# Gated linear attention into an expert layer: the third unit's k product moves to VectorE and the first 300 entries of the order are written anew

## The chip, the cores and the metric

The kernel runs on 1 core of one Trainium2 chip. The metric is the device time of one execution in microseconds. A core has five engines with a queue each: TensorE (PE in the profile, with its weight loads as PEld), VectorE (DVE), ScalarE (ACT), GpSimd (POOL) and SyncE (SP, which here only issues transfers). Every queue is worked in its order, and the engines meet by semaphores.

## The reference, cut to what matters

Gated linear attention over 4 batches, 8 heads, 768 positions and 48 channels, then a two-layer expert network over the 3072 x 384 result:

```python
for t in range(S):
    state = f[:, :, t, :, None] * state + np.einsum('bhd,bhe->bhde', k[:, :, t], v[:, :, t])
    y[:, :, t] = np.einsum('bhd,bhde->bhe', q[:, :, t], state)
...
h = x @ w_in                       # 3072 x 384 by 384 x 2048
relu6 = np.clip(h + 3.0, 0.0, 6.0)
g = h * relu6 / 6.0
return g @ w_out                   # 2048 x 384
```

Here `f` is the sigmoid of `f_logit`, and `x` is `y` with the heads side by side.

## The kernel before, in words

**Units.** The recurrence is done in chunks of 128 positions: 4 batches by 6 chunks are 24 units, named 0 to 23; units 0 to 3 are the first chunks of the four batches. For a unit, `load` brings the gates (258.5 KB), `loadk` and `loadq` bring k and q (256 KB each; from unit 2 on `loadq` brings both, 512 KB) and `loadv` brings v (200 KB). `gate` is the sigmoid on ScalarE. On VectorE `back` scans the gates backwards (L433), `kmul` multiplies k by that scan (L446), `rend` takes a reciprocal (L451), `fwd` scans forwards (L457) and `qmul` multiplies q (L463). On TensorE `tk` transposes k (L529), `att` makes the scores (L510), `kv` the unit's sum of k and v (L550), `qs` the part that comes from the state before (L585), `av` the part from the scores (L601), and `xs` takes back the rounded part of the result (L626). Between these, `ktok`, `carry0`, `carry1`, `xh` and `xl` are copies out of PSUM on ScalarE for units 0 to 3 (L536, L563, L570, L622, L634), and `mask` multiplies the scores on VectorE (L517). `hole` issues two small transfers that move rows of the result within SBUF (L643).

**Weights.** Each of 16 slices of the two weight matrices is brought by `ld` (768 KB) and split by `cy`, `z` and `high` on ScalarE (L296, L287, L316) and `mid`, `dif`, `top` and `lowi`/`lowo` on VectorE (L300, L307, L311, L319).

**Expert network.** Group c holds the 512 results of the units 4c to 4c+3. For group 0 the first slices are done by halves: `mm1a.f` needs units 0 and 1 alone, `mm1b.f` units 2 and 3 (L846); then `relua`/`relub` on ScalarE (L855), `ga`/`gb` on VectorE (L859) and `mm2a`/`mm2b` on TensorE (L864). Later slices and groups use L678, L727, L738 and L790. `mm1a` multiplies by the high half of a slice's weights in its first six products and by the low half, which `lowi` makes, in the last three.

**Where the order comes from.** Nothing is scheduled while it runs. The string `ORDER` lists 1565 entries, and the program issues them in that order, so each engine's queue is the list's entries for that engine. The string `ON_POOL` names the entries that go to GpSimd in place of VectorE. An entry `warm.n` multiplies a tile of zeros, n blocks of 128 columns, into an unused PSUM bank (L1089): these are the blank products. A number behind a product's name picks its PSUM bank; two steps of a unit that use the same pair of banks wait for each other in the order of the list.

**Queue of SP.** All input transfers and the holes stand in one queue. A transfer waits there for its buffer: `load.3` for `fwd.0`, which frees the first of three gate buffers, and `hole.0` for `xl.0`. Whatever stands behind waits with it.

Of the kernel before, what the change touches and what calls it, by code (L numbers as in the profile page):

```python
# [58 lines left out]
rend.2 cy.0 load.3 warm.3 kv.1.3 z.0 mid.0 loadq.2 kmul.2 gate.3 end.2 back.3 ld.1 carry0.1 warm.1 qs.1.0 dif.0 fwd.2
qmul.2 top.0 xl.0 carry1.1 loadq.3 loadv.2 av.1 hole.0 tk.2.4 rend.3 xh.1 xs.1 xl.1 z.1 warm.5 att.2.2 kmul.3 cy.1  # L60
mid.1 fwd.3 ktok.2 high.0 warm.4 kv.2.1 carry0.2 end.3 tk.3.4 ktok.3 mask.2 load.4 gate.4 qs.2.0 hole.1 av.2 xh.2
carry1.2 lowi.0 mm1a.0.4 relua.0 dif.1 qmul.3 top.1 high.1 ga.0 loadv.3 xs.2 att.3.2 mask.3 kv.3.1 ld.2 carry0.3
carry1.3 lowi.1 xl.2 loadq.4 warm.1 qs.3.2 av.3 xh.3 mm1a.1.4 cy.2 xs.3 xl.3 relua.1 z.2 back.4 kmul.4 rend.4 fwd.4
ga.1 decay.4 mm2a.0 qmul.4 load.5 gate.5 tk.4.1 mm2a.1 ktok.4 loadv.4 ld.3 cy.3 z.3 hole.2 mid.2 dif.2 top.2 att.4.2
kv.4.3 hole.3 mm1b.0.0 high.2 back.5 mid.3 relub.0 loadq.5 mm1b.1.1 relub.1 lowi.2 gb.0 dif.3 kmul.5 rend.5 gb.1
mm1a.2.4 mm1b.2.0 top.3 mm2b.0 mm2b.1 fwd.5 tk.5.1 relua.2 relub.2 gb.2 qmul.5 ld.4 z.4 cy.4 mid.4 mm2b.2 high.3 ktok.5
lowi.3 ga.2 mm1b.3.0 load.6 gate.6 loadq.6 dif.4 back.6 top.4 load.7 mm1a.3.4 ld.5 relub.3 mm2a.2 relua.3 ga.3 high.4
gb.3 cy.5 z.5 mask.4 mm2a.3 lowi.4 mm1a.4.1 relua.4 rend.6 ld.6 mm1b.4.4 relub.4 loadv.6 gate.7 loadq.7 mm2b.3 carry0.4
kmul.6 fwd.6 mid.5 ga.4 dif.5 z.6 qmul.6 top.5 cy.6 tk.6.1 ktok.6 mm2a.4 back.7 ld.7 decay.5 high.5 qs.4.2 decay.6
att.5.0 gb.4 av.4 kv.6.1 carry1.4 lowi.5 mm1.5.4 mask.5 mm2b.4 carry0.6 xh.4 z.7 xl.4 mid.6 dif.6 kmul.7 carry1.6  # L70
loadv.5 kv.5.3 ld.8 relu.5 g.5 mm2x.5 cy.7 top.6 high.6 cy.8 rend.7 tk.7.0 mid.7 dif.7 load.8 lowi.6 carry0.5 top.7
mm1.6.4 ktok.7 qs.5.2 fwd.7 qmul.7 high.7 loadv.7 relu.6 g.6 z.8 decay.7 att.6.0 ld.9 lowi.7 gate.8 av.5 cy.9 z.9
mask.6 mm1.7.4 relu.7 mid.8 dif.8 top.8 mid.9 carry1.5 dif.9 high.8 low.8 mm2x.6 mm1.8.0 g.7 loadq.8 ld.10 top.9 xh.5
cy.10 relu.8 high.9 back.8 rend.8 mm2x.7 ld.11 xl.5 g.8 att.7.2 z.10 cy.11 qs.6.0 kv.7.3 mid.10 load.10 loadv.8 av.6
dif.10 low.9 top.10 z.11 mid.11 gh.8 mm1.9.4 ld.12 ld.14 xh.6 xl.6 gl.8 mm2.8 dif.11 high.10 low.10 relu.9 g.9 cy.12
mm1.10.1 top.11 mask.7 kmul.8 carry0.7 gh.9 gl.9 hole.4 relu.10 high.11 mm2.9 carry1.7 g.10 low.11 z.12 mid.12 ld.13
dif.12 top.12 cy.13 gh.10 gl.10 tk.8.1 ktok.8 mm1.11.0 z.13 high.12 qs.7.2 mm2.10 av.7 loadq.9 ld.15 kv.8.3 decay.8
relu.11 mid.13 dif.13 low.12 loadv.9 mm1.12.1 g.11 gh.11 xh.7 top.13 carry0.8 high.13 xl.7 hole.7 gl.11 relu.12 z.14
z.15 low.13 fwd.8 qmul.8 mm2.11 g.12 gh.12 mm1.13.4 relu.13 g.13 cy.14 gh.13 gl.13 gl.12 mm2.12 cy.15 qs.8.2 mid.14
dif.14 att.8.0 mask.8 lowo.0 top.14 high.14 hole.6 hole.5 mm1.16.4 load.9 mid.15 mm1.17.1 relu.16 carry1.8 relu.17  # L80
dif.15 ws1.0 g.16 mm1.20.0 g.17 loadq.11 low.14 gate.10 xtop.0 gate.9 mm1.18.1 load.11 top.15 relu.18 loadq.10 back.9
high.15 gh.16 av.8 back.10 mm1.14.4 g.18 mm2.13 lowo.4 gh.17 relu.14 low.15 g.14 gh.14 mm1.15.1 mm1.19.4 lowo.6 gh.18
kmul.9 gl.18 rend.9 relu.15 g.15 lowo.3 gh.15 gl.14 gl.15 tk.9.1 lowo.5 lowo.1 mm2.14 fwd.9 mm2.15 gl.16 ktok.9 gl.17
# [1173 lines left out]
```

## Time and profile before

| | us |
|---|---|
| median of 3 runs | 455.48 (455.41 to 456.07) |
| the profiled execution, its own time | 455.55 |
| its span from the first to the last instruction | 453.8 |
| TensorE busy in the span | 446.9 |
| VectorE busy | 357.8 |
| ScalarE busy | 231.5 |
| GpSimd busy | 19.8 |

The 1.75 us between the span and the execution's own time lie before the first and behind the last instruction. The profile says of each engine when it worked, how long it stood idle before an instruction, and what released it; the chain of waits goes back from the last instruction to what released each step. Times in the rows are us from the span's start.

### The profile page before, as it was taken

Reading aid. Unit: us, or ns where it says so; the run is one execution under the profiler, and the core shown is the slowest. Engines: PE = TensorE matmul, PEld = TensorE weight load, DVE = VectorE, ACT = ScalarE, POOL = GpSimd, SP = SyncE. Lnnn points to the kernel's source line nnn. Section 1 sums busy time; section 2 is a strip of 40 time slices with the busy share of each in tenths; the row PEclk is TensorE's granted clock in tenths of the full one; section 3 lists DMA queues with packets and bytes.
Section 4 is the critical chain, followed back from the end, with each engine's and each line's share of the span. In section 5 each row is a group of like instructions: output and inputs, shape, how many; then the busy total and the mean of one; then the engine's idle time right before and its main releaser. Section 6 shows DMA issues by size and latency. Waiting matters only on the chain.

```text
span 453.8 us, 12556 instructions
## 1 busy us (share of the span) xinstructions
PE 446.9 (98%) x5447; PEld 290.3 (64%) x5447; DVE 357.8 (79%) x639; ACT 231.5 (51%) x393; POOL 19.8 (4%) x31
## 2 busy tenths in 40 slices
...
GB/s 285 248 264 408 173 224 228 196 172 0 73 139 66 190 20 110 58 6 118 91 0 85 109 129 1 30 135 1 2 10 1 7 28 1 1 116 2 1 0 74
DMA packets 25819, 43.18 MB, mean 95 GB/s; under 512 B 2592, under 2 KB 17440, under 8 KB 25760
## 3 DMA queue, kind: packets, MB, share of 16 engines
q1 hardware_dynamic: 24160, 41.56, 27.0%
...
q14 instruction: 16, 0.13, 0.1%
...
## 4 chain that ended last, share of the span: by engine, by line
PE 95%; DMA 2%; DVE 1%; POOL 1%; issue 0%; SPq 0%; ACT 0%; DVEq 0%; POOLq 0%
PE o L727 36%; PE pair L790 16%; PE single L790 9%; PE pair L678 7%; PE single L678 5%; PE o L864 3%; PE pair L510 3%; PE pair L585 3%; PE pair L601 3%; PE pair L550 2%; PE o L738 2%; DMA qkf<-qk 2%; PE pair L529 2%; PE pair L880 1%; PE o_half L880 1%; PE single L846 1%
## 5 line engine op out<-in xcount | busy, mean ns | idle before, releaser
L727 PE MATMUL o<-gg,weight 128*128 128x512 f16 x744 | 173.5, 379 | 0.0
L727 PEld LDWEIGHTS <-weight 128*128 128x128 f16 x744 | 71.7, 98 | 73.7
L790 PEld LDWEIGHTS <-weight 128*128 128x128 f16 x672 | 65.0, 98 | 13.2
L790 PE MATMUL pair<-xmem,wide 128*128 128x256 f16 x384 | 51.4, 273 | 0.2 <-issue 0.2
L701 ACT ACTIVATE gg<-raws 128x512 f16<-128x512 f32 x64 | 38.5, 624 | 22.8 <-PE o_half L880 7.2
L790 PE MATMUL single<-xmem,weight 128*128 128x256 f16 x384 | 49.8, 273 | 0.0
L819 ACT ACTIVATE raws<-pair,half 128x512 f32<-128x512 f32 x32 | 21.5, 684 | 43.0 <-PE pair L790 34.0
L790 PEld LDWEIGHTS <-wide 128*128 128x128 f16 x384 | 36.8, 98 | 9.2 <-DVE single L805 0.7
L819 ACT ACTIVATE raws<-single,half 128x512 f32<-128x512 f32 x32 | 22.0, 687 | 38.5 <-PE single L790 37.6
L678 PEld LDWEIGHTS <-weight 128*128 128x128 f16 x243 | 23.1, 98 | 26.7 <-issue 0.3
L790 PE MATMUL pair<-xmem,weight 128*128 128x256 f16 x288 | 36.5, 273 | 0.0
L711 DVE TENSOR_TENSOR gg<-raws,gg 128x512 f16<-128x512 f32 x48 | 31.9, 682 | 5.2 <-ACT gg L701 5.1
L824 DVE SCALAR_TENSOR_TENSOR raws<-raws,single 128x512 f32<-128x512 f32 x32 | 21.8, 682 | 17.6 <-ACT raws L819 17.6
L678 PE MATMUL pair<-xmem,weight 128*128 128x512 f16 x144 | 33.2, 379 | 0.0
L805 DVE TENSOR_TENSOR pair<-pair,raws 128x512 f32<-128x512 f32 x16 | 11.2, 697 | 26.7 <-PE pair L790 23.7
L457 DVE TENSOR_TENSOR_SCAN suffix<-gates,rend 112x516 f32<-112x516 f32 x24 | 29.7, 1236 | 1.2 <-POOL qkf L446 1.1
L824 DVE SCALAR_TENSOR_TENSOR raws<-raws,pair 128x512 f32<-128x512 f32 x32 | 21.4, 681 | 10.9 <-ACT raws L819 10.8
L433 DVE TENSOR_TENSOR_SCAN suffix<-gates,unit 112x516 f32<-112x516 f32 x23 | 28.0, 1222 | 0.2 <-ACT gates L427 0.2
L678 PE MATMUL single<-xmem,weight 128*128 128x512 f16 x99 | 23.2, 380 | 0.0
L688 ACT ACTIVATE tg<-pair,half 128x512 f32<-128x512 f32 x16 | 10.9, 689 | 19.4 <-PE pair L678 16.2
L701 ACT ACTIVATE gg<-tg 128x512 f16<-128x512 f32 x24 | 14.4, 626 | 9.0 <-DVE tg L692 5.2
L517 DVE TENSOR_TENSOR a<-pair,causal 128x512 f32<-128x512 f32 x24 | 16.3, 683 | 1.3 <-PE pair L550 1.0
(135 smaller groups left out, 638.4 us busy)
## 6 DMA issues: line engine op xcount, KB each, us to landing
...
qkf<-qk SPq DMA_DIRECT2D x22, 512.0 KB, 4.8
gates<-fg SPq DMA_DIRECT2D x23, 258.5 KB, 3.2
...
outT<-os SPq DMA_DIRECT2D x11, 256.0 KB, 2.9
qkf<-qk SPq DMA_DIRECT2D x4, 256.0 KB, 4.1
...
```

Source lines behind the costliest of these rows:

```text
L433: nc.vector.tensor_tensor_scan(flat(sf)[:, ::-1], gt[:, 1:][:, ::-1], flat(unit)[:, ::-1], 0.0, op0=ALU.mult, op1=ALU.add,)
L457: nc.vector.tensor_tensor_scan(flat(sf), gt[:, :NP * (C + 1)], flat(rend), 0.0, op0=ALU.mult, op1=ALU.add,)
L510: nc.tensor.matmul(d["at"][HC * odd:HC * (odd + 1), e, 2 * n + c], t[rs, 1, n, c, odd], t[rs, 0, n, c, odd], start=not growing[at], stop=T ...
L517: nc.vector.tensor_tensor(d["a"].rearrange("r p e t -> r e p t"), d["at"], causal.unsqueeze(1).unsqueeze(1).broadcast_to([128, 2, NP, HC]) ...
L585: nc.tensor.matmul(d["y"][to:to + m, odd, n, cs], before[rs, p, :m], t[rs, 0, n, c, odd], start=alone and (odd, e) not in seen, stop=False ...
L678: nc.tensor.matmul(h, win[:, f, a, k * 128:(k + 1) * 128], g["xt"][:, k, :g["n"] // C, b], start=i == 0, stop=i == 3 * KT - 1,)
L701: nc.scalar.activation(as_t(d, 0), d["t"], AF.Copy)
L711: engine("gl", int(g["name"]) * NF + f).tensor_tensor(as_t(d, 1), d["t"], as_t(d, 0), op=ALU.subtract)
L727: nc.tensor.matmul(g["o"][m], wout[:, f, a, m * 128:(m + 1) * 128], g[f]["gg"][:, b], start=f == 0 and i == 0, stop=f == NF - 1 and i == 2 ...
L790: nc.tensor.matmul(to[:, n * 256:(n + 1) * 256], weights(q, n, a), g["wide"][:, :, block - 3, b], start=fresh and count == 1, stop=count = ...
L819: nc.scalar.activation(to, src, AF.Relu, bias=half, scale=RISE)
L824: nc.vector.scalar_tensor_tensor(to, to, TOP, src, op0=ALU.min, op1=ALU.mult)
```

## The change: what it does

`kmul.2`, the product of k with the backward scan for unit 2, is struck from `ON_POOL`, so it runs on VectorE. The first 309 entries of `ORDER` are the same entries in another order, but for the blank products: after the first ten blocks there were 23 in nine places, now 18 in nine places. The 1256 entries behind are untouched.

```diff
 ON_POOL = """
-kmul.2 decay.4 kmul.6 lowi.5 kmul.7 decay.7 lowi.7 kmul.8 gl.9 decay.8 gl.11 qmul.8 gl.12 lowo.0 low.14
+decay.4 kmul.6 lowi.5 kmul.7 decay.7 lowi.7 kmul.8 gl.9 decay.8 gl.11 qmul.8 gl.12 lowo.0 low.14
 """.split()
 ORDER = """
-load.0 loadh.0 gate.0 gateh.0 back.0 backh.0 loadk.0 load.1 loadv.0 loadq.0 rend.0 end.0 kmul.0 fwd.0 gate.1 back.1
+load.0 loadh.0 gate.0 gateh.0 loadk.0 back.0 backh.0 rend.0 kmul.0 warm.10 end.0 fwd.0 load.1 gate.1 back.1 loadq.0
...
```

**VectorE, from unit 1's `kmul` on.** Before (`rend.1`, `kmul.1`, `mask.0`, `fwd.1`, `qmul.1`, `back.2`, `mask.1`, `rend.2`, `mid.0`, `back.3`, `dif.0`, `fwd.2`):

```order
L451 RECIPROCAL rend<-suffix_79 112x4
L446 TENSOR_TENSOR qkf_184<-qkf_184,suffix_79 112x512
L517 TENSOR_TENSOR a_217<-pair_70,causal 128x2x4x64
L457 SCALAR_TENSOR_TENSOR suffix_79<-gates_78,rend 112x516
L463 TENSOR_TENSOR qkf_184<-qkf_184,suffix_79 112x512
L433 SCALAR_TENSOR_TENSOR suffix_81<-gates_80,unit 112x516
L517 TENSOR_TENSOR a_271<-pair_70,causal 128x2x4x64
L451 RECIPROCAL rend<-suffix_81 112x4
L300 TENSOR_SCALAR raws<-top_274 128x768
L433 SCALAR_TENSOR_TENSOR suffix_77<-gates_76,unit 112x516
L307 TENSOR_TENSOR top_274<-top_274,raws 128x768
L457 SCALAR_TENSOR_TENSOR suffix_81<-gates_80,rend 112x516
```

and now (`rend.1`, `kmul.1`, `fwd.1`, `mask.0`, `back.2`, `qmul.1`, `rend.2`, `kmul.2`, `fwd.2`, `mask.1`, `qmul.2`, `back.3`):

```order
L451 RECIPROCAL rend<-suffix_79 112x4
L446 TENSOR_TENSOR qkf_154<-qkf_154,suffix_79 112x512
L457 SCALAR_TENSOR_TENSOR suffix_79<-gates_78,rend 112x516
L517 TENSOR_TENSOR a_228<-pair_70,causal 128x2x4x64
L433 SCALAR_TENSOR_TENSOR suffix_81<-gates_80,unit 112x516
L463 TENSOR_TENSOR qkf_154<-qkf_154,suffix_79 112x512
L451 RECIPROCAL rend<-suffix_81 112x4
L446 TENSOR_TENSOR qkf_224<-qkf_224,suffix_81 112x512
L457 SCALAR_TENSOR_TENSOR suffix_81<-gates_80,rend 112x516
L517 TENSOR_TENSOR a_311<-pair_70,causal 128x2x4x64
L463 TENSOR_TENSOR qkf_224<-qkf_224,suffix_81 112x512
L433 SCALAR_TENSOR_TENSOR suffix_77<-gates_76,unit 112x516
```

`kmul.2` (the second L446) is new here, `fwd.1` stands ahead of `mask.0`, `fwd.2` ahead of `mask.1`, and the first slice's `mid.0` and `dif.0` stand behind `mask.2`. Further down, `back.4` stands ahead of `ga.0` and `lowi.1`, where it stood behind them.

**SP, from the ninth transfer to the first `hole`** (`qkf` is k and q, `gates` the gates, `v` v, `raws` a weight slice, `xmem` a hole). Before:

```order
L408 DMA gates_80<-fg 128x517
L419 DMA qkf_184<-qk 128x512
L283 DMA raws<-w 128x3072
L423 DMA v_268<-v 128x400
L408 DMA gates_76<-fg 128x517
L412 DMA qkf_304<-qk 128x1024
L283 DMA raws<-w 128x3072
L412 DMA qkf_327<-qk 128x1024
L423 DMA v_329<-v 128x400
L643 DMA xmem<-xmem 16x3x256 x2
```

and now:

```order
L419 DMA qkf_154<-qk 128x512
L408 DMA gates_80<-fg 128x517
L412 DMA qkf_224<-qk 128x1024
L423 DMA v_253<-v 128x400
L408 DMA gates_76<-fg 128x517
L283 DMA raws<-w 128x3072 x2
L423 DMA v_377<-v 128x400
L412 DMA qkf_415<-qk 128x1024
L643 DMA xmem<-xmem 16x3x256 x2
```

Unit 2's k and q (`loadq.2`, the first row of 128x1024) come tenth in the queue, ahead of the first weight slice, where they came thirteenth; the two first slices stand together behind `load.3`.

**TensorE, unit 0's scores and the part from the state.** Before:

```order
L510 MATMUL pair_70<-qkf_137 64x64 [waits DMAHW5_49,DVE_49,Activation_49]
L510 MATMUL pair_70<-qkf_137 64x64 x15
L585 MATMUL pair_71<-qkf_137,middle_102 64x64 [waits Pool_49]
L585 MATMUL pair_71<-qkf_137,middle_102 64x64 x7
L1089 MATMUL idle<-blank 128x128
L601 MATMUL pair_71<-a_217,v_140 64x64 [waits PE_49,DVE_49]
```

and now:

```order
L510 MATMUL pair_70<-qkf_135 64x64 [waits DMAHW4_49,DVE_49]
L510 MATMUL pair_70<-qkf_135 64x64 x15
L1089 MATMUL idle<-blank 128x128
L585 MATMUL pair_71<-qkf_135,middle_102 64x64 [waits Activation_49,Pool_49]
L585 MATMUL pair_71<-qkf_135,middle_102 64x64 x7
L529 MATMUL single<-ident,qkf_154 128x112 [waits DMAHW6_49,DVE_49]
```

The wait on ScalarE (for `carry0.0`) has gone from `att.0` to `qs.0`: `carry0.0` now comes behind `att.0` in the list, and as both use the same pair of banks, it waits for `att.0`. Unit 1's transposition (`tk.1`, L529) stands ahead of `av.0`.

## Rows read from the trace of the kernel before

**Rows 1.** The page's head, and its part 1: busy time by engine

```profile
span 453.8 us, 12556 instructions
PE 446.9 (98%) x5447; PEld 290.3 (64%) x5447; DVE 357.8 (79%) x639; ACT 231.5 (51%) x393; POOL 19.8 (4%) x31
```

**Rows 2.** Windows: length, busy us by engine, granted clock, DMA share, GB/s

```profile
5.00:30.00 25.00, 23.25 (x580) 16.52 (x580) 23.25 (x36) 17.21 (x37) 2.93 (x2) 1.00 0.83 309
30.00:450.00 420.00, 419.70 (x4865) 271.95 (x4863) 331.96 (x594) 211.95 (x354) 14.17 (x13) 1.00 0.25 82
```

**Rows 3.** The chain of waits, 0 to 110 us: start, length, what

```profile
7.53 7.28 DMA qkf<-qk
...
14.95 2.43 POOL qkf L446
```

**Rows 4.** Timeline of TensorE and its loads: start, length, what, idle before

```profile
9.37 0.44 PE L585 MATMUL pair<-qkf,middle 48*64 48x64 f32 x16
...
14.16 1.33 PE L550 MATMUL pair<-v,ktok 64*64 64x48 f32 x48
...
21.10 0.91 PE L550 MATMUL pair<-v,ktok 64*64 64x48 f32 x48
...
28.08 1.16 PE L846 MATMUL single<-xmem,weight 128*128 128x256 f16 x9
```

**Rows 5.** Timeline of VectorE: `kmul.1`, `fwd.2`, `lowi.1`

```profile
8.79 0.66 DVE L446 TENSOR_TENSOR qkf<-qkf,suffix 112x512 f32<-112x512 f32 x1
...
17.41 1.23 DVE L457 TENSOR_TENSOR_SCAN suffix<-gates,rend 112x516 f32<-112x516 f32 x1 [1.07 <-POOL qkf L446]
...
26.45 0.55 DVE L319 TENSOR_TENSOR weight<-wide,weight 128x384 f16<-128x384 f32 x1
```

**Rows 6.** VectorE by line to 28.2 us: count, busy us, mean ns, idle before

```profile
L457 DVE TENSOR_TENSOR_SCAN suffix<-gates,rend 112x516 f32<-112x516 f32 x4 | 4.9, 1230 | 1.1 <-POOL qkf L446 1.1
L433 DVE TENSOR_TENSOR_SCAN suffix<-gates,unit 112x516 f32<-112x516 f32 x4 | 4.9, 1222 | 0.2 <-ACT gates L427 0.2
L517 DVE TENSOR_TENSOR a<-pair,causal 128x512 f32<-128x512 f32 x4 | 2.7, 687 | 0.3 <-PE pair L510 0.3
...
L446 DVE TENSOR_TENSOR qkf<-qkf,suffix 112x512 f32<-112x512 f32 x4 | 2.7, 672 | 0.0
```

**Rows 7.** DMA issues at 4.57 (`loadq.1`), 7.16 (`load.3`), 7.53 (`loadq.2`): KB, us to landing

```profile
qkf<-qk SPq DMA_DIRECT2D x1, 256.0 KB, 4.7
...
gates<-fg SPq DMA_DIRECT2D x1, 258.5 KB, 5.2
...
qkf<-qk SPq DMA_DIRECT2D x1, 512.0 KB, 7.3
```

**Rows 8.** Timeline of ScalarE: `carry0.0`, `z.1`, `cy.1`, `xl.3`

```profile
8.27 0.33 ACT L563 ACTIVATE middle<-pair 112x192 f32<-112x192 f32 x1 [1.21 <-PE pair L550]
...
18.86 0.91 ACT L287 ACTIVATE wide<-raws 128x768 int32<-128x768 uint32 x1
19.68 0.91 ACT L296 ACTIVATE top<-raws 128x768 int16<-128x768 int16 x1
...
29.50 0.59 ACT L634 ACTIVATE xmem<-pair 112x512 f16<-112x512 f32 x1
```

**Rows 9.** Timeline of TensorE's weight loads inside `kv.1`: start, length, idle before

```profile
14.15 0.65 PEld L550 LDWEIGHTS pair<-v,ktok 64*64 64x64 f32 x35 [0.55 <-issue]
15.05 0.31 PEld L550 LDWEIGHTS pair<-v,ktok 64*48 64x48 f32 x13 [0.24 <-issue]
```

**Rows 10.** DMA queues in 12.5 to 13 and in 16.5 to 17 us: packets, MB, share

```profile
q8 instruction: 1, 0.02, 12.0%
...
q8 instruction: 1, 0.02, 15.7%
```

**Rows 11.** Window 16 to 18 us, and SP's first `hole`

```profile
16.00:18.00 2.00, 1.69 (x53) 1.31 (x54) 0.93 (x2) 1.17 (x3) 1.37 (x1) 1.00 0.34 119
...
16.38 2.20 SPq L643 DMA_DIRECT2D xmem<-xmem  x2
```

More of the change, by code (lines that the diff above doesn't have):

```diff
@@ L59 @@
[L59 to L83, printed above, removed]
@@ new lines @@
+att.2.2 z.0 back.3 av.1 xh.1 warm.3 xs.1 z.1 mask.2 xl.1 mid.0 rend.3 end.3 dif.0 top.0 cy.1 loadv.2 warm.3 kv.2.1
+carry0.2 warm.1 qs.2.0 high.0 loadq.3 kmul.3 av.2 tk.3.4 fwd.3 carry1.2 mid.1 qmul.3 dif.1 xh.2 hole.0 ktok.3 lowi.0
+att.3.2 ld.2 cy.2 loadv.3 load.4 hole.1 gate.4 xs.2 kv.3.1 carry0.3 top.1 mm1a.0.4 high.1 mask.3 loadq.4 back.4 relua.0
+ga.0 lowi.1 load.5 xl.2 rend.4 carry1.3 qs.3.2 av.3 xh.3 mm1a.1.4 relua.1 ld.3 xs.3 xl.3 loadv.4 kmul.4 fwd.4 z.2 ga.1
+qmul.4 mm2a.0 hole.2 hole.3 mid.2 loadq.5 dif.2 top.2 ld.4 tk.4.1 ktok.4 mm2a.1 carry1.1 loadq.6 gate.5 cy.3 back.5
```

146 lines of the change are left out of this document (83 added, 63 removed).

## The prediction

> **What bounds the kernel now.** I read the page's head first: TensorE is busy 446.9 us of a span of 453.8 [rows 1]. The windows say where it is not: from 30 to 450 us it stands idle 0.3 us in all, while from 5 to 30 us it is busy 23.25 of 25 [rows 2], and 23 blank products stand among that work. So from 30 us on the time is a queue of TensorE that never runs dry, and the opening sets when that queue starts. The chain of waits names the opening's links: unit 2's k and q are issued at 7.53 and land 7.28 later, GpSimd multiplies k for 2.43, and TensorE can only then transpose it [rows 3].
>
> That gives a mark by which both orders can be compared: the start of `mm1a.1`, the first-half product of slice 1, at 28.08 [rows 4]. The same products of TensorE stand ahead of it in both orders, blanks apart, and behind it the old order has no idle time worth a name. The time changes by as much as this mark moves, plus what idle time the new order brings in behind it.
>
> **The change on VectorE.** Before, the chain from `kmul.1` at 8.79 to the end of `lowi.1` at 27.00 takes 18.21 [rows 5]. Of that 1.07 is `fwd.2` waiting for GpSimd's `kmul.2` [rows 5], about 0.3 `mask.0` waiting for `att.0`, and 0.15 one `back` [rows 6]: 1.5 in all. The new order adds `kmul.2` (0.67 by its line, 0.60 from start to start) and puts `back.4` ahead (1.22 by its line, 1.17 net) [rows 6]. If VectorE never waits, `lowi.1` ends at 8.79 + 18.21 - 1.5 + 0.60 + 1.17 = 27.3, and `ga.0`, which frees the bank for `mm1a.1`, half a microsecond earlier, at 26.8. `lowi.1` itself is wanted only by the seventh of that step's nine products.
>
> Does VectorE have to wait for `loadq.2`, now that a late landing stops its whole queue? The nine transfers that now stand ahead of `loadq.2` are the nine that ended with `loadq.1` before, and that one landed at 4.57 + 4.7 = 9.3. The 512 KB behind it take up to 2.4 (before, `loadq.2` landed at 7.53 + 7.3 = 14.8 behind `load.3` at 7.16 + 5.2 = 12.4) [rows 7]: 11.7. VectorE comes to `kmul.2` at 8.79 + 0.60 (`kmul.1`) + 1.2 (`fwd.1`) + 0.6 (`mask.0`) + 1.2 (`back.2`) + 0.7 (`qmul.1`, `rend.2`) = 13.1. So it does not wait, with 1.4 to spare, and `kmul.2` is done at 13.7 where GpSimd ended at 17.38. The 2.43 on GpSimd itself vanish; nothing else there is due before 29.
>
> **The change on TensorE and ScalarE.** `carry0.0` ran at 8.27, ahead of the scores [rows 8]; now it waits for `att.0`, which ends at 9.6, so `qs.0` starts at about 10.2 in place of 9.37 [rows 4]. That costs nothing by itself: `av.0` needs `mask.0`, which now ends at 11.2, behind `fwd.1`. From there, with steps as long as in the old order (0.45 for `qs`, 0.5 `tk`, 0.65 `att` and `av`, 0.85 net for `kv`, about 0.55 for a copy on ScalarE) and 0.15 from a releaser to a start: `att.1` at 13.2 (`qmul.1`), `tk.2` 13.95, `kv.1` 14.45, `qs.1` 15.95 (`carry0.1`), `att.2` 16.4 (`qmul.2`), `av.1` to 17.7. Then ScalarE sets the pace: `xh.1` to 18.3, `z.1` (0.91 [rows 8], some 0.8 net) to 19.1, and only then `xl.1` to 19.65, which `kv.2` has to wait for, since both use one bank. `kv.2` starts at 19.85 in place of 21.10 [rows 4]: 1.25 earlier. From `kv.2` to the mark the old order takes 28.08 - 21.10 = 6.98; the new one has the same products and waits some 0.15 more (`kv.3` for `ktok.3`), so `av.3` ends at 27.0. But `relua.0` stands on ScalarE behind `cy.2`, `gate.4`, `carry0.3` and `high.1`; it ends at 26.65, `ga.0` at 27.15, and the mark comes at 27.3. That is 0.8 earlier than before. The five blanks less are no gain of their own: they filled waits.
>
> Behind the mark `mm1b.0` needs the last `hole`, and this needs `xl.3`, at 29.50 before [rows 8] and 1.4 behind the mark's start. In the new order `relua.1` stands ahead of it: 0.05 given back, so 0.75 is left. Later places where VectorE could be late (`lowi.2`, `ga.2`, `lowi.3`, `ga.3`, `lowi.6`) come out in time by 0.2 to 1.0 by the same sums, as VectorE is itself some 0.9 ahead there: I cost them at nothing. If that cover fails, each pays its own lateness once.
>
> **The instruction read.** Inside `kv.1` TensorE stands idle 0.24 for nothing but "issue", at 14.8 to 15.05 [rows 9], and `kv.1` takes 1.33 where `kv.2` takes 0.91 [rows 4]. The only thing in flight that fits is a 16 KB read in the instruction queue, begun between 12.5 and 13 while the DMA engines were full [rows 10]. I take it that TensorE ran out of code. By counting instructions in both orders the same place comes 25 instead of 35 matmuls into `kv.1`, at 14.45 + 0.43 = 14.9. If the read arrives as before, at 15.05, that costs 0.15; if it is asked for by TensorE's own progress, it may be late by what `qs.0` is late, 0.83, and costs 15.9 - 14.9 = 1.0. Nothing lets me choose, so I take the middle, 0.55; `mask.2` has 0.2 of slack against it, so 0.35 goes on to the mark.
>
> The Trainium skill, "Runtime: NRT & Kernel Launch", section "Instruction fetch mechanics", says that the sequencer reads the next 16 KiB block with a queue of its own while it executes the current one, and that a crossing is mostly hidden. The packet's size agrees; the idle 0.24 [rows 9] speaks against "hidden" in this place. By the page the read would cost 0 and the sum would be -0.75.
>
> **The sum.** -0.75 + 0.35 = -0.4 against the profiled execution's 455.55: 455.15. The median of the runs shown is 0.07 below that execution, so **455.1**. A measurement of this kernel can tell about 0.2%, 0.9 us, from no change; this forecast is the same as before by that measure.
>
> **Rivals.**
> - *The opening runs as smoothly as its order allows.* The read is hidden, and `top.1` to `ga.0` keep ahead of TensorE, so that `av.3` and not `ga.0` sets the mark: 27.0, or 1.1 earlier, 454.4. For it: in the sums `ga.0` misses by only 0.3, and VectorE alone would have it at 26.8. Against it: every link has to be on time. 0.26. (The page of the Trainium skill named above, "Runtime: NRT & Kernel Launch", would have the read so; the gap before is the evidence against it.)
> - *The reads get slower, because the pause goes.* Before, SP waited for `xl.0` until 16.38 to issue the first `hole`, the transfers ran out, and the DMA share fell to 0.34 in 16 to 18 us; TensorE's second read, begun between 16.5 and 17, fell into that pause [rows 10, 11]. Now `xl.0` is done about 13.9 (`av.0` from 11.4, then `xh.0`, `xs.0`, `xl.0`), SP goes on, and the pause closes. The first read then costs the full 1.0, less 0.2 of slack; the second, wanted inside `kv.2` at 20.1 and asked for at 15.9, may take as long as from `qs.0`'s start at 9.37 to the first one's 15.05, 5.7, and arrive at 21.6: 1.5 more. -0.75 + 0.8 + 1.5 = +1.55: 457.0 at most, 456.5 if the second loses 1.0. It is slower by over 0.2% once both together put more than 1.65 on the path. For it: 0.24 was lost already. Against it: no later step before shows such a gap, and the packet itself takes one engine only 0.12 x 16 x 0.5 = 0.96 us [rows 10]. 0.12.
> - *`kmul.2` now blocks VectorE.* If `loadq.2` lands as late as before, at 14.8, VectorE idles 1.7 at 13.1 with `fwd.2`, `mask.1` and `qmul.2` behind it: -0.4 + 1.7 = +1.3, 456.4. It decides from a landing at 13.1 on, and is slower by over 0.2% from 14.4. Against it: 1226 KB less stand ahead of it. 0.06.
> - *Nothing is gained*, as VectorE's places behind 30 us give the 0.4 back one by one: 455.5. 0.10.
>
> **How the numbers follow.** Forecast 0.46, no gain 0.10: within 0.2%, 0.56. Smooth: 0.26 faster. The two mishaps: 0.18 slower. The range reaches from just under the smooth case to the lighter end of the slow ones: 454.3 to 456.4.
>
> **What would show it.** Right: `kmul.2` on VectorE near 13.1 with no wait before it; `fwd.2` at 13.7; `kv.2` near 19.9 behind `xl.1`; `mm1a.1` near 27.3 to 27.6; no idle time of TensorE from 30 to 450 us. The read shows as an "issue" gap in `kv.1`, 0.15 to 1.0 long. Wrong: an idle VectorE before `kmul.2` (a DMA as releaser); "issue" gaps in `kv.1` and `kv.2` that sum over 1.65; `mm1a.1` before 27.1; or idle time of TensorE before L846, L864 and L678 behind 30 us with VectorE or ScalarE as releaser.

## The result and the profile after

The changed kernel takes 458.9 us in the median of 6 runs (458.02 to 460.69) beside 455.43 for the kernel before: a ratio of 1.0082, 95% interval 1.0064 to 1.0099. It is 3.5 us slower. 455.1 was predicted, between 454.3 and 456.4. The profiled execution of the changed kernel took 458.96, its span 457.2, against 455.55 and 453.8; the sums below are made between these two.

First the windows, as in [rows 2], with single microseconds added. Columns: stretch, length, busy us of TensorE, its weight loads, VectorE, ScalarE and GpSimd (count of instructions), TensorE's granted clock, DMA share, GB/s.

```profile
5.00:30.00 25.00, 22.26 (x515) 15.77 (x514) 21.24 (x31) 14.86 (x30) 0.00 (x0) 0.86 0.83 307
30.00:450.00 420.00, 419.25 (x4896) 271.85 (x4899) 333.37 (x587) 213.46 (x357) 17.45 (x14) 1.00 0.25 80
...
17.00:18.00 1.00, 1.00 (x41) 0.70 (x33) 1.00 (x3) 1.00 (x2) 0.00 (x0) 1.00 0.83 240
20.00:21.00 1.00, 0.09 (x3) 0.00 (x0) 0.96 (x2) 0.40 (x1) 0.00 (x0) 1.00 0.74 272
22.00:23.00 1.00, 0.81 (x18) 0.48 (x18) 1.00 (x2) 0.96 (x2) 0.00 (x0) 1.00 0.62 173
23.00:24.00 1.00, 0.93 (x32) 0.95 (x32) 0.86 (x3) 0.10 (x1) 0.00 (x0) 0.52 1.03 412
28.00:29.00 1.00, 1.00 (x12) 0.69 (x7) 0.28 (x1) 0.67 (x2) 0.00 (x0) 0.50 0.03 10
30.00:31.00 1.00, 0.91 (x42) 0.70 (x44) 0.31 (x1) 0.82 (x2) 0.00 (x0) 1.00 0.00 0
```

The granted clock between 5 and 30 us is 0.86 where it was 1.00: TensorE all but stands from 20 to 21 us, runs on at full speed, and at 23.0 the clock falls to 0.50, that is to 1.2 of 2.4 GHz, until 29.9. The DMA engines, which had a pause before [rows 11], are 0.83 busy in 17 to 18 us.

TensorE's timeline, to be read against [rows 4] (start, length, line, operation, count, idle time before and its releaser). Idle time marked "issue" is time in which the engine waited for nothing that the profile shows; a *stop*, below, is such idle time of TensorE.

```profile
14.76 0.91 PE L550 MATMUL pair<-v,ktok 64*64 64x48 f32 x48
...
19.55 0.55 PE L550 MATMUL pair<-v,ktok 64*64 64x48 f32 x20 [0.21 <-ACT xmem L634]
21.27 0.66 PE L550 MATMUL pair<-v,ktok 64*64 64x48 f32 x28 [1.17 <-issue]
...
23.07 1.13 PE L601 MATMUL pair<-a,v 64*64 64x64 f32 x32 [0.18 <-DVE top L307]
...
26.73 1.53 PE L550 MATMUL pair<-v,ktok 64*64 64x48 f32 x48
...
31.24 1.16 PE L846 MATMUL single<-xmem,weight 128*128 128x256 f16 x9
```

`kv.1` runs through. `kv.2` starts at 19.55 behind ScalarE's `xl.1`, as planned, and stops for 1.17 after 20 of its 48 matmuls. At the lower clock `kv.3` takes 1.53 where `kv.2` took 0.91 before. The mark, `mm1a.1`, comes at 31.24 in place of 28.08.

VectorE's and SP's timelines (`kmul.2` and `fwd.2`; the first `hole`, `ld.2`, `loadv.3`, `load.4`):

```profile
13.01 0.66 DVE L446 TENSOR_TENSOR qkf<-qkf,suffix 112x512 f32<-112x512 f32 x1
13.70 1.23 DVE L457 TENSOR_TENSOR_SCAN suffix<-gates,rend 112x516 f32<-112x516 f32 x1
...
14.33 1.36 SPq L643 DMA_DIRECT2D xmem<-xmem  x2
15.73 0.58 SPq L283 DMA_DIRECT2D raws<-w  x1
16.36 0.43 SPq L423 DMA_DIRECT2D v<-v  x1
16.89 0.38 SPq L408 DMA_DIRECT2D gates<-fg  x1
```

The DMA view of 12.5 to 13 and of 18.5 to 19 us has the first two instruction reads, as [rows 10]:

```profile
q8 instruction: 1, 0.02, 12.6%
...
q8 instruction: 1, 0.02, 11.1%
```

The second read began at 18.8; before, it began at 16.9 [rows 10].

**Where the time went.** The profiled executions differ by 3.41: the mark by 3.16, and 0.25 behind it, where one wait of 0.30 for VectorE's `th` is new:

```profile
55.97 2.10 PE L678 MATMUL single<-xmem,weight 128*128 128x512 f16 x9 [0.30 <-DVE th L859]
```

Before, TensorE reached matmul 20 of `kv.2` at 21.10 + 20 x 0.017 = 21.44 and needed 28.08 - 21.44 = 6.64 from there to the mark. Now it passed that place at 21.27, only 0.17 earlier, although `kv.2` had started 1.55 earlier: the stop took the lead. From there it needed 31.24 - 21.27 = 9.97 for the same products: 3.33 more. -0.17 + 3.33 = 3.16. The stretch at 0.50 is 6.8 long, and half of it, 3.4, is work not done.

### The profile page after: what moved, and what is told of

It is laid out like the page before. It is cut to its first block, busy times and chain, and to the rows that moved or that the text cites. A ratio compares the mean times of both kernels' runs of the same rounds, so it can differ in the third digit from the quotient of the medians.

```text
span 457.2 us, 12557 instructions
## 1 busy us (share of the span) xinstructions
PE 448.9 (98%) x5441; PEld 292.0 (64%) x5445; DVE 359.4 (79%) x640; ACT 231.3 (51%) x393; POOL 20.2 (4%) x30
## 3 DMA queue, kind: packets, MB, share of 16 engines
q1 hardware_dynamic: 24160, 41.56, 27.3%
## 4 chain that ended last, share of the span: by engine, by line
PE 88%; DVE 6%; DMA 2%; issue 2%; ACT 1%; SPq 0%; ACTq 0%
PE o L727 35%; PE pair L790 16%; PE single L790 9%; PE pair L678 7%; PE single L678 4%; PE pair L510 3%; PE pair L601 2%; PE pair L585 2%; PE pair L550 2%; PE o L738 2%; DMA raws<-w 1%; PE pair L529 1%; PE pair L880 1%; PE o_half L880 1%; DMA v<-v 1%
```

## The experiments

**The theories.** *Queue*: TensorE's 16 KB read of its own code waits behind the transfers in flight; the new order closes the pause, so the second read is late, TensorE stands, and for that the clock falls. *Progress*: a read takes its six microseconds (15.05 - 9.37 = 5.7 for the first one before, counted from the start of `qs.0`) whatever the transfers do, and TensorE is simply there too early. *Blanks*: the clock falls because the new order has five blanks less, stop or no stop. Later runs ask what the order would be worth without all that. Times are medians with the ratio to the kernel before, run beside them; each run also has a mean granted clock, which is 0.998 to 1.000 where it held, and 0.988 to 0.996 where it fell for a while. The kernel before is not wholly free of this: its clock fell in 2 of the 122 runs beside these experiments (457.09 and 457.17 us).

**The pause put back** (the changed kernel; SP, and `cy.2` on ScalarE).

```diff
-SP:  hole.0 ld.2 loadv.3 load.4 hole.1 loadq.4
+SP:  hole.0 loadv.3 hole.1 load.4 ld.2 loadq.4
-ACT: ktok.3 cy.2 gate.4 ... xh.3 relua.1
+ACT: ktok.3 gate.4 ... xh.3 cy.2 relua.1
```

> The changed kernel with SP's queue behind `hole.0` put back nearly as before: `ld.2` (768 KB) and `load.4` (258 KB) stand behind `hole.1`, only `loadv.3` (200 KB) between the two holes; `cy.2`, which reads what `ld.2` brings, stands behind `xh.3`, as before. Queue theory (TensorE's second instruction read waits behind the transfers that SP issues from 15.7 us on; the idle time it causes in `kv.2` then lowers the granted clock): the read's packet begins at 16.5 to 17.5 in place of 18.8, no "issue" gap over 0.2 us in `kv.2`, granted clock 1.00 from 20 to 30 us, `mm1a.1` at 27.2 to 27.7, 454.5 to 455.2 us. Progress rival (the read takes its six microseconds whatever the transfers do, and TensorE is simply there too early): the gap of 1.2 stays, `mm1a.1` near 31, 458.5 to 459 us. Blanks rival (the clock falls because the new order has five blank products fewer, not because of the gap): no gap, but a stretch at 0.50 between 20 and 30 us, 457 to 458 us.

456.2 us, ratio 1.0032 (1.0012 to 1.0052). The clock held in 9 of 12 runs, median 455.78, and fell in 3, median 459.32. In the profiled run:

```profile
16.10 0.49 PE L550 MATMUL pair<-v,ktok 64*64 64x48 f32 x19 [0.30 <-issue]
...
20.46 0.91 PE L550 MATMUL pair<-v,ktok 64*64 64x48 f32 x48 [0.21 <-ACT xmem L634]
...
27.95 1.14 PE L846 MATMUL single<-xmem,weight 128*128 128x256 f16 x9
```

The second read begins at 18.2, 2.1 after TensorE entered its block in place of 3.6, and `kv.2` runs through; the clock is 1.00 from 20 to 30 us with the same 18 blanks. That speaks against Progress and against Blanks, with two reserves: `kv.2` also starts 0.9 later than in the changed kernel, and of the 3 runs that lost their clock no trace shows why. The packet is not as early as expected, the first read costs 0.30 in `kv.1`, and the runs whose clock held are still not faster than the kernel before.

Why they are not, the same trace shows. The mark comes at 27.95, 0.13 earlier than before, but this execution takes 456.28, 0.73 longer. Behind the mark TensorE now waits for VectorE's `th`, and from 30 to 110 us it is idle 0.89 where it was idle 0.08 (TensorE's timeline of this run, then the window in the kernel before and in this run):

```profile
31.29 1.56 PE L864 MATMUL o<-th,wide 128*128 128x256 f32 x6 [0.29 <-DVE th L859]
...
53.29 2.10 PE L678 MATMUL single<-xmem,weight 128*128 128x512 f16 x9 [0.29 <-DVE th L859]
```

```profile
30.00:110.00 80.00, 79.92 (x988) 49.17 (x987) 72.83 (x126) 57.65 (x87) 14.17 (x13) 1.00 0.57 204
30.00:110.00 80.00, 79.11 (x983) 48.39 (x982) 73.28 (x125) 57.51 (x87) 16.46 (x13) 1.00 0.59 211
```

**Half a pause** (`load.4` between the two holes).

```diff
-SP:  hole.0 loadv.3 hole.1 load.4 ld.2
+SP:  hole.0 loadv.3 load.4 hole.1 ld.2
```

> As `pause`, but `load.4` stands ahead of `hole.1`, so that 458 KB and not 200 KB are issued between the two holes. Queue theory: the second read begins between the 16.5 to 17.5 of `pause` and the 18.8 of the changed kernel, near 17.5 to 18.2; a gap in `kv.2` of 0 to 0.7 us; 454.5 to 455.8 us if the clock holds, 457 to 458 if it falls for that gap. Progress rival: the gap of 1.2 stays, 458.5 to 459 us.

455.66, ratio 1.0017 (1.0001 to 1.0033): clock held in 7 of 10 runs, median 455.50, fell in 3, median 458.63. The profiled run was one of these three, and its clock fell for the first read, not for the second:

```profile
14.28 0.66 PE L550 MATMUL pair<-v,ktok 64*64 64x48 f32 x29
17.03 0.76 PE L550 MATMUL pair<-v,ktok 64*64 64x48 f32 x19 [2.09 <-issue]
```

How late the first read is differs from run to run: its stop in `kv.1` was 0 to 2.09 long in the profiles of the changed kernel, `again`, `pause`, `on_pool` and `half_pause`, whose order up to there is all but the same.

**TensorE idle for ScalarE** (`pause`, less two blanks).

```diff
-PE:  av.1 warm.3 xs.1 warm.3 kv.2
+PE:  av.1 xs.1 kv.2
```

> The kernel of `pause` without the two blanks of 384 columns on both sides of `xs.1`, so that TensorE stands idle there for some 0.8 and 0.8 us, waiting for ScalarE and not for instructions. If idle time of TensorE of whatever cause lowers the granted clock: a stretch at 0.50 that begins between 19 and 23 us and lasts near 6.8 us, as in the changed kernel, and 2.5 to 3.5 us more than `pause`: 457.3 to 458.5 us. If only a wait for instructions does it, or one piece has to be over a microsecond: clock 1.00, and the time of `pause` within 0.3 us.

457.35, ratio 1.0050 (1.0036 to 1.0065); the clock fell in all 4 runs. TensorE's timeline, then the windows of 20 to 21, 21 to 22 and 22 to 24 us:

```profile
17.90 0.43 PE L625 MATMUL pair<-xmem,less 112*112 112x256 f16 x2 [0.72 <-ACT xmem L621]
19.18 1.23 PE L549 MATMUL pair<-v,ktok 64*64 64x48 f32 x48 [0.85 <-ACT xmem L633]
```

```profile
20.00:21.00 1.00, 0.90 (x30) 0.66 (x29) 0.96 (x2) 0.48 (x3) 0.00 (x0) 1.00 0.17 41
21.00:22.00 1.00, 0.82 (x41) 0.71 (x45) 1.00 (x3) 0.61 (x1) 0.00 (x0) 0.94 0.42 69
22.00:24.00 2.00, 2.00 (x47) 1.58 (x43) 2.00 (x4) 1.36 (x4) 0.00 (x0) 0.50 0.84 243
```

Two waits for ScalarE of 0.72 and 0.85 come before the clock falls at 21.9, when TensorE is back at work; the median is 1.6 us over that of the runs of `pause` whose clock held. The run is not free of a late read: `kv.2` is 1.23 long, as its weight loads stop inside it.

```profile
19.86 0.43 PEld L549 LDWEIGHTS pair<-v,ktok 64*64 64x64 f32 x24 [0.24 <-issue]
```

So this run alone does not tell waits from reads; `idle_before`, below, does.

**One part undone** (`kmul.2` on GpSimd again).

```diff
+ON_POOL: kmul.2
```

> The changed kernel, its order untouched, with `kmul.2` back on GpSimd: the one part undone. GpSimd starts it at 13.1 and takes about 2.4, so `fwd.2` and `tk.2` come about 1.3 us later and `kv.2` starts near 20.7. Queue theory: the read still begins near 18.8 to 19.3, bound by the transfers, and is there at 21.3 to 21.8, when TensorE wants it at 21.1; the gap falls to 0 to 0.7, the clock holds, and the kernel is FASTER than with `kmul.2` on VectorE by 2 to 3.5 us: 455.3 to 457 us. Progress rival: the read is asked for 1.3 later too, the gap of 1.2 and the low clock stay, 459 to 460 us.

457.51, ratio 1.0042 (1.0019 to 1.0065): clock held in 2 of 7 runs (455.44, 455.52), fell in 5, median 458.90. The premise was wrong: GpSimd took it at 12.38 and needed 1.54 in place of 2.43, so `tk.2` came no later (13.97, in the changed kernel 14.22). The profile has two stops, 0.94 in `kv.1` and 0.98 in `kv.2`. Little follows for the theories, as TensorE was not held back. The median is lower than the changed kernel's (458.9, and 460.49 in its repetition, below), and the clock held in 2 of 7 runs where it held in none of 10; nothing in the trace ties that to the engine that does `kmul.2`, and whether it matters in the new order stays open.

**The weight transfers cut, in both orders.**

```diff
-    nc.sync.dma_start(out=raw[:, ...], in_=w[f]...)
+    rows = 32 if f < 3 else 128
+    nc.sync.dma_start(out=raw[:rows, ...], in_=w[f][:rows]...)
```

> The changed kernel with the transfers of the first three weight slices (`ld.0`, `ld.1`, `ld.2`) cut to 32 of 128 rows, 192 KB in place of 768 KB each; the other rows hold a constant that GpSimd writes at the start, so the output of these slices is not the reference's. Nothing else moves. If the instruction reads wait behind transfers: both early reads begin within some 2 us of being asked for, no "issue" gap in `kv.1` or `kv.2`, granted clock 1.00 from 5 to 30 us, `mm1a.1` near 27.3 and 454.3 to 455.2 us, 3.5 to 4.5 under the changed kernel. If the reads take their six microseconds anyway: the gap of 1.2 in `kv.2` and the low clock stay, 458 to 459 us.

> The same cut of `ld.0` to `ld.2` in the kernel before (output of these slices not the reference's). Its reads were all but covered, so it should stay within 0.4 us of the kernel before: 454.8 to 455.3 us. The difference to `light_after` is then what the new order is worth where no read is late: -0.4 to -0.8 us if the sum of the prediction without its read term holds, nothing or a loss if later steps of VectorE give the lead back.

`light_after` 458.08, ratio 1.0053 (1.0029 to 1.0078), `light_before` 456.94, ratio 1.0046 (1.0023 to 1.0069). Inconclusive as to the first read: up to 16 us the DMA engines stayed nearly as busy (share 0.97 from 2 to 16 us at 297 GB/s in `light_after`, beside 1.02 at 364 in the changed kernel), and GpSimd, which writes the constants, is busy 9.77 of these 14 us in place of 1.51. Both profiles have a stop in `kv.1`, 1.65 and 1.16, so even the old order, all its 23 blanks in place, loses time for a read that comes late, and in 3 of its 6 runs the clock as well. In `light_before` (TensorE's timeline, and the windows of 17 to 18 and of 18 to 19 us):

```profile
15.94 0.43 PE L554 MATMUL pair<-v,ktok 64*48 64x48 f32 x13 [1.16 <-issue]
```

```profile
17.00:18.00 1.00, 0.92 (x48) 0.72 (x45) 1.00 (x1) 0.47 (x2) 0.00 (x0) 1.00 0.00 0
18.00:19.00 1.00, 1.00 (x13) 0.84 (x6) 0.97 (x3) 0.60 (x1) 0.00 (x0) 0.54 0.14 39
```

After 16 us the load is gone here, and no second read makes a stop.

**Less in flight ahead of the reads.**

```diff
-SP:  loadq.0 loadv.0 ... load.3 ld.0 ld.1 loadv.2 loadq.3 hole.0 ld.2 loadv.3 load.4 hole.1
+SP:  loadv.0 loadq.0 ... load.3 loadv.2 loadq.3 ld.0 hole.0 loadv.3 ld.1 load.4 hole.1 ld.2
-ACT: z.1 xl.1 end.3 cy.1 carry0.2   ktok.3 cy.2 ... xh.3
+ACT: xl.1 end.3 z.1 carry0.2 cy.1   ktok.3 ... xh.3 cy.2
```

> The changed kernel with the whole work, but SP's queue made so that little is in flight when TensorE asks for its next block: `ld.1` goes from 7.9 us to behind `hole.0` (some 15.5), `ld.2` behind `hole.1` (some 19.5), `loadv.2`, `loadq.3` ahead of `ld.0`, `loadv.0` ahead of `loadq.0`; on ScalarE `z.1` and `cy.1` go behind `xl.1`, `cy.2` behind `xh.3`. Queue theory: first read back by 14.7, second asked for near 15 and back by 18.5; no gap over 0.2 us, clock 1.00, `mm1a.1` at 26.5 to 27.4; 454.2 to 455.0 us, the fastest of all. If the later weight slices hold ScalarE up instead (`z.1` waiting for `ld.1` past 19.5): 455.2 to 456 us with the clock at 1.00. Progress rival: gaps as in the changed kernel, 458 to 459 us.

459.42, ratio 1.0106 (1.0065 to 1.0146): the clock fell in all 6 runs, and three reads in a row were late.

```profile
15.95 0.49 PE L549 MATMUL pair<-v,ktok 64*64 64x48 f32 x19 [1.16 <-issue]
22.62 0.66 PE L549 MATMUL pair<-v,ktok 64*64 64x48 f32 x28 [1.62 <-issue]
28.56 1.03 PE L549 MATMUL pair<-v,ktok 64*48 64x48 f32 x38 [1.58 <-issue]
```

A miss by over 4 us. The profiled run, 463.16, is one of two over 463; besides the three stops it has a wait of 1.85 for VectorE at 48.7. The transfers were not fewer, only later: SP issued `loadv.3`, `ld.1` and `load.4` at 15.1 to 16.6, when TensorE asked for its second block, and the packet began at 20.2, when they were done (DMA share 0.20 in 20 to 21 us).

**The changed kernel again.**

> The changed kernel once more, on the chip and beside the runs of these three. If the late read is the rule for this order: mean granted clock 0.991 to 0.994 in nearly every run and 458 to 460 us. If it is a matter of the single run: some runs at 1.00 and 454.5 to 456 us among them.

460.49, ratio 1.0097 (1.0076 to 1.0119), the clock at 0.988 to 0.993 in all 4 runs. With the first set that is 10 of 10. In this profile `kv.2` stands 2.25, the read having begun at 20.7.

**The old order with the pause closed**, **the old order with less blanks**, **the first part of the change alone**:

```diff
 closed_before (the kernel before)
-SP:  loadv.2 hole.0 load.4 hole.1 loadv.3 ld.2
+SP:  loadv.2 load.4 loadv.3 ld.2 hole.0 hole.1
 idle_before (the kernel before)
-PE:  xs.1 warm.5 att.2 warm.4 kv.2
+PE:  xs.1 att.2 kv.2
 kmul_alone (the kernel before)
-ON_POOL: kmul.2
```

> The kernel BEFORE, every engine's order untouched but SP's: `load.4`, `loadv.3` and `ld.2` (1226 KB) stand ahead of `hole.0`, so that the transfers no longer run dry at 16.5 us. Queue theory: TensorE asks for its second block at 15.05 as it did, but the packet begins at 18 to 20 us in place of 16.93 and is of use 1.4 after its end, at 20.3 to 22.4, where TensorE wants it at 21.38: a gap of 0 to 1.0 in `kv.2`, with the low clock where the gap is long; 455.2 to 458.5 us, and more spread between runs than the 0.9 of the kernel before. Progress rival (a read takes its time whatever the transfers do): the packet at 16.9, no gap, 455.0 to 455.4 us.

> The kernel BEFORE without `warm.5` and `warm.4`, the nine blanks that stand ahead of `att.2` and `kv.2`: TensorE is idle there some 1.2 and 1.1 us, waiting for VectorE and ScalarE, with every transfer and read as before. If idle time of TensorE alone lowers the granted clock: a stretch at 0.50 that begins between 19 and 24 us, and 457 to 459 us. If the low clock belongs to waits for instructions or to the new order: clock 1.00 and 455.0 to 455.5 us.

> The kernel BEFORE with `kmul.2` on VectorE, its order untouched: the first part of the change alone. `loadq.2` still lands at 14.8, so `kmul.2` runs at 14.9 to 15.6 and the queue behind it (`back.3`, `dif.0`, `fwd.2`) starts at 15.6; `fwd.2` at 17.3 in place of 17.41, `tk.2` behind `av.1` at 17.2 in place of 17.43. TensorE's code and the transfers are unchanged, so the reads are: 454.8 to 455.3 us, the same as before. Rival (the product on GpSimd was the opening's brake by itself): 454.3 to 454.7.

`closed_before`: 457.01, ratio 1.0049 (1.0031 to 1.0067). Nothing but transfers has moved, and the second read, asked for at about the same time, no longer begins in 16.5 to 17 but in 19 to 19.5 us, where the DMA view has

```profile
q8 instruction: 1, 0.02, 11.9%
```

and TensorE's timeline a late third read, in `kv.3`:

```profile
26.71 0.90 PE L550 MATMUL pair<-v,ktok 64*48 64x48 f32 x46 [0.39 <-issue]
```

The old `kv.2` wants the second read late enough to be slowed only to 1.19; the third costs 0.39. The clock held in 4 of the 5 runs. This is Queue without the fall of the clock, in the old order.

`idle_before`: 458.12, ratio 1.0065 (1.0050 to 1.0081), the clock low in all 4 runs. TensorE's timeline, then the windows of 21 to 22 and of 24 to 28 us:

```profile
19.25 0.69 PE L509 MATMUL pair<-qkf 48*64 48x64 f32 x32 [1.01 <-DVE qkf L462]
20.95 1.26 PE L549 MATMUL pair<-v,ktok 64*64 64x48 f32 x48 [1.01 <-ACT ktok L535]
```

```profile
21.00:22.00 1.00, 1.00 (x48) 1.00 (x48) 1.00 (x2) 0.63 (x1) 0.00 (x0) 0.66 0.55 144
24.00:28.00 4.00, 4.00 (x63) 3.02 (x66) 1.58 (x3) 1.90 (x5) 0.00 (x0) 0.50 1.01 386
```

Nine blanks less, no stop but the first read's 0.17 in `kv.1` (which `small2`, below, has too, with its clock held), and 2.9 us lost: in the old order the blanks, which only fill waits, are what keeps the clock.

`kmul_alone`: 455.03, ratio 0.9996 (0.9987 to 1.0006): no change, the clock held in all 10 runs. `kmul.2` ran at 15.20 behind its transfer, as expected.

**Three more tries to keep the new order and its reads**, from the changed kernel (with `cy.2` as in `pause`):

```diff
 quiet
+SP:  loadv.0 loadq.0 ... load.3 loadv.2 loadq.3 ld.0 ld.1 hole.0 loadv.3 load.4 hole.1 ld.2
 sp_of_before
+SP:  the first 21 transfers in the sequence of the kernel before
 mixed
+SP:  as sp_of_before, with loadq.2 ahead of loadv.1 and load.3
```

> The try at a version that beats both: the changed kernel with SP's queue as in `half_pause` (`ld.2` behind `hole.1`, `cy.2` behind `xh.3`), `loadv.0` ahead of `loadq.0` so that `kv.0` does not wait for v, and `loadv.2`, `loadq.3` ahead of `ld.0`, `ld.1`, so that fewer of the long weight rows stand ahead of the first read. If the first read's lateness comes from the weight rows queued just ahead of it: packet at 12 to 13, gap in `kv.1` under 0.3, no low clock in most runs, median 454.6 to 455.1. If any transfers do it: packet at 13 to 14.5 as in `half_pause`, gaps of 0.3 to 2 in `kv.1`, some runs at 457 to 459, median 455.3 to 457.

> The changed kernel with SP's first 21 transfers in the sequence of the kernel before (`cy.2` behind `xh.3`, as `ld.2` comes late again). If SP's sequence makes the first read late: packet at 12.3 to 12.9 as in the kernel before and its three variants, no gap over 0.3 in `kv.1`, second read begun by 17, low clock in no run or one. `kmul.2` then waits on VectorE for `loadq.2`, which lands near 14.8: 1.7 idle at 13.1, `tk.2` and `kv.1` 1.5 later than in the changed kernel, `kv.2` near 21: 455.0 to 456.0. If the engines' order makes it late: packet at 13 to 14.5, gaps, clock low in several runs, 456.5 to 459.

> As `sp_of_before`, with `loadq.2` ahead of `loadv.1` and `load.3`: it lands near 13.5 to 14, `kmul.2` waits some 0.5 to 0.9, `kv.2` near 20.2, its second half wanted at 20.6 where the second read is of use near 19.6. If SP's sequence is the cause and the new order is worth what the prediction's sum without the read says (-0.75, less 0.5 for this wait): clock 1.00, no gap over 0.3, 454.5 to 455.1. If moving one transfer brings the late read back: packet at 13 to 14.5, gaps of 0.5 to 2, 455.5 to 458.

`quiet` 456.95, ratio 1.0035 (1.0021 to 1.0049), a stop of 1.57 in `kv.1` that the clock survived in the profiled run; `sp_of_before` 458.36, ratio 1.0072 (1.0058 to 1.0087); `mixed` 456.94, ratio 1.0038 (1.0024 to 1.0051), a stop of 1.85. None is faster; each came out as the second, worse case of what was expected. The first reads began at 14.0, 13.3 and 14.1. In the profiles of all kernels with the new opening the first read begins at 12.3 to 14.6, in those with the old one at 12.4 to 13.4, the latest of these in `light_before`. With SP's old sequence it began at 13.3 and made no stop in the one run that has a trace, but that is the only one of four whose clock held; so that sequence is no cure, and why the new opening's first read is later and less regular is not settled.

**The old opening, with `kv.2` moved up.**

```diff
 small (the kernel before; kmul.2 on VectorE)
-DVE: rend.2 mid.0 back.3 dif.0 fwd.2 qmul.2 top.0 rend.3 kmul.3 mid.1 fwd.3 mask.2
+DVE: rend.2 mid.0 kmul.2 fwd.2 qmul.2 back.3 dif.0 top.0 rend.3 kmul.3 mask.2 mid.1 fwd.3
-PE:  tk.2 xs.1 warm.5 att.2 warm.4 kv.2 tk.3 qs.2 av.2 mm1a.0
+PE:  tk.2 xs.1 att.2 warm.2 kv.2 warm.2 qs.2 tk.3 av.2 warm.2 mm1a.0
-ACT: xh.1 xl.1 z.1 cy.1 ktok.2 high.0 carry0.2
+ACT: xh.1 ktok.2 xl.1 z.1 carry0.2 cy.1 high.0
-SP:  load.3 loadq.2 ... hole.0 load.4 hole.1 loadv.3
+SP:  loadq.2 load.3 ... hole.0 loadv.3 load.4 hole.1
 small2: SP as before; high.0 ahead of carry0.2; lowi.0 fwd.3 mid.1
 small3: loadq.2 load.3 again; carry0.2 high.0 cy.1
```

> The kernel BEFORE up to unit 2, with `kmul.2` on VectorE directly ahead of `fwd.2`, `qmul.2`; `loadq.2` one place ahead; `ktok.2` ahead of `z.1`, `cy.1`; `mask.2` ahead of `mid.1`, `fwd.3`; `loadv.3`, `load.4` between the holes; 17 blanks in place of 23 blocks. TensorE then wants `kv.2` at 19.1 in place of 21.10, its second block at 19.4, where the read (begun 16.9 before) is of use near 19.5. If the reads keep up: no gap over 0.3, `mm1a.1` 0.7 to 1.2 earlier than 28.08, clock 1.00, 454.1 to 454.8: faster than both. If the earlier `kv.2` only turns into a wait for the second read: `issue` in `kv.2` of 0.5 to 1.5, 455.0 to 456, with the low clock in some runs 457 to 458. If the later steps of VectorE give the lead back: 454.9 to 455.3 at clock 1.00.

> As `small`, with SP's transfers wholly in the sequence of the kernel before, `high.0` ahead of `carry0.2` on ScalarE and `lowi.0`, `fwd.3` ahead of `mid.1` on VectorE. `hole.1` then issues at 19.2 to 20.4 and lands near 22.9; `kv.2` near 19.8 with its second block wanted at 20.1, where the second read is of use at 19.5 to 19.9; `mm1a.0` at 22.9 to 23.2 in place of 23.73 and `mm1a.1` at 27.2 to 27.7 in place of 28.08. If the lead then holds: clock 1.00 and 454.5 to 455.0, faster than the kernel before by 0.3 to 0.8. If later steps give it back: 455.0 to 455.4. If the earlier `kv.2` meets a late read in some runs: these at 457 to 460, the median 455.3 or more.

> As `small2`, with `carry0.2` ahead of `high.0` again and `loadq.2` one place ahead of `load.3`, so that `kmul.2` waits some 0.3 in place of 0.99. `kv.2` at 19.4 to 19.8, `qs.2` at 20.9 in place of 21.87, `mm1a.0` near 22.9, `mm1a.1` at 27.3 to 27.6 in place of 28.26. If the lead holds to the end: 454.5 to 455.0 at clock 1.00, ratio under 0.9990. If later steps give it back: 455.1 to 455.5. If the second block is now wanted before its read is of use (19.9): a gap of 0.3 to 1 in `kv.2`, 455 to 456 and some runs at a low clock.

455.83, ratio 1.0011 (0.9993 to 1.0029); 455.42, ratio 0.9994 (0.9985 to 1.0003); 455.51, ratio 1.0003 (0.9994 to 1.0012). The clock held in 33 of 34 runs. `small2` starts `kv.2` 1.69 earlier than [rows 4] and has it whole, and still its mark comes at 28.26:

```profile
19.41 0.91 PE L550 MATMUL pair<-v,ktok 64*64 64x48 f32 x48
...
21.87 0.46 PE L585 MATMUL pair<-qkf,middle 48*64 48x64 f32 x16 [0.92 <-ACT middle L563]
...
28.26 1.16 PE L846 MATMUL single<-xmem,weight 128*128 128x256 f16 x9
```

In each of the three the lead ended in another wait: 1.12 for the second `hole`'s transfer (`small`), 0.92 for `carry0.2` behind `high.0` (`small2`), and in `small3` 0.44 for the `hole` and 0.21 for `carry0.3`. None beats the kernel before.

**What the second read shows over the kernels.** "Entered" is where TensorE began the block before: the end of the stop in `kv.1`, or, in the changed kernel, which has none there, counted back by 128 matmul records from the stop in `kv.2`; the packet's start is the trace's; "stop" is idle time in front of the code that was read.

| kernel | entered | packet begun | stop in `kv.2` |
|---|---|---|---|
| before | 15.05 | 16.93 | none |
| small2 | 14.95 | 16.83 | none |
| pause | 16.10 | 18.17 | none |
| half_pause | 17.03 | 19.24 | none |
| light_before | 15.94 | 18.33 | none |
| quiet | 16.36 | 18.86 | 0.19, of the weight loads alone |
| mixed | 16.64 | 18.56 | none |
| light_after | 17.25 | 20.54 | none |
| on_pool | 16.10 | 19.42 | 0.98 |
| changed | 15.17 | 18.81 | 1.17 |
| light_queue | 15.95 | 20.17 | 1.62 |
| again | 15.79 | 20.68 | 2.25 |

Where transfers ran out or were few, the packet began 1.9 to 2.5 after the block was entered; where SP had issued more by then, 3.3 to 4.9. The 1.9 to 2.5 are not the transfers' doing alone: in `light_before` the DMA engines were 0.04 busy in 16 to 17 us and 0.00 in 17 to 18, and the packet still began 2.4 after the block was entered. What that time is spent on no run tells. TensorE went on 1.6 after the end of the packet in the changed kernel (19.70 to 21.27) and 1.3 after it in the kernel before's first read (13.74 to 15.05).

## Why the prediction was wrong

**What held.** The mark is the place where the difference arises: it moved by 3.16 of 3.41. VectorE's chain: `kmul.2` at 13.01 for 13.1 forecast, with no wait, and `fwd.2` at 13.70 for 13.7. TensorE's and ScalarE's chain to `kv.2`: 19.55 behind `xl.1`, for 19.85. The chain from `kv.2` to the mark, seen where the clock held: 27.95 - 20.46 = 7.49 in `pause`, for 27.3 - 19.85 = 7.45 forecast.

**The step that failed is "The instruction read".** It priced one read, in `kv.1`, at 0.55, and the second at nothing. In the profiled run the first made no stop, which was luck (0 to 2.09 in the profiles here); the second took 1.17 and with it nearly the whole lead of 1.55. This stood in the text as the rival "The reads get slower, because the pause goes", with its place right (wanted at 20.1: TensorE stood from 20.10) and its size nearly (back at 21.6: it was 21.27, 6.1 after the block was entered, for 5.7; 1.5 lost: 1.17). That rival was given 0.12. The argument against it, that no later step before shows such a gap, counted for nothing, as the text itself said that before, the second read fell into the pause; in `closed_before`, without the pause, the second read is late in the old order too, and TensorE stops 0.39 for the third. The other argument, that the packet takes one engine only 0.96, had the packet's size right (0.89, from 18.81 to 19.70), but the lateness lies in the 3.6 that pass before the packet begins. The pause closes by the order that the change sets, not by chance; the late read should have been a term of the sum. One count in that step was off without weight: the block ends 29 matmuls into `kv.1` (the stops of `again`, `pause`, `half_pause` and `on_pool`), not 25.

**The term that was missing is the clock.** Neither the sum nor a rival had a row for a granted clock under 1.00, since [rows 2] shows none. It cost 3.33 at the mark, the largest single term, and carried the result out of the range: without it this execution would have taken some 455.6. The range's slow end, 456.4, lay just under that rival's price for late reads alone. The sentence on the five blanks ("they filled waits") was right about the time they cost and blind to what else they do: `idle` and `idle_before` lose 1.6 and 2.9 us for blanks that cost nothing (the first with a small late read in it). In the changed kernel it was the stop and not the missing five: `pause`, with the same 18, keeps its clock in 9 of 12 runs, and `light_before`, with all 23, loses it behind a stop of 1.16.

**The cover behind the mark failed too.** Without the read the forecast was -0.75, with the places where VectorE could be late behind 30 us costed "at nothing". In the changed kernel one of them took 0.30. In `pause` the mark is 0.13 earlier although the first read took 0.30 in `kv.1`, and then TensorE stands idle 0.81 more from 30 to 110 us than before. `pause` differs from the changed kernel in SP's queue and in the place of `cy.2`, so the size need not be the same there. This is what the rival "Nothing is gained" describes, which was given 0.10, and more than the 0.4 that it has VectorE's places give back. It fits the medians of the runs whose clock held and whose order was the new one, 455.78 (`pause`) and 455.50 (`half_pause`). What the changed kernel's own order of transfers would take with both reads on time was not measured. The nearest is the profiled run of `sp_of_before`, with no stop and the clock at 1.00, but with VectorE waiting for `loadq.2`: 456.54. In the old opening, `small2` and `small3`, with prompt reads and `kv.2` up to 1.69 earlier, come out equal to the kernel before, and `kmul.2` on VectorE by itself is worth nothing there (`kmul_alone`).

The Trainium skill, "Runtime: NRT & Kernel Launch", section "Instruction fetch mechanics", has a 16 KiB crossing mostly hidden. The size agrees with the packets; the stops of 1.17 in the changed kernel, 2.25 in its repetition and 2.09 in `half_pause` speak against "hidden" in openings whose DMA engines are nearly full. The measurement decides.
